# State times w_in as eight 64x32 tiles of the array, two banks at a time, in a fused attention and snake-MLP kernel

## The chip, the cores and the metric

The kernel runs on one core of a Trainium2 chip. The metric is the device time of one execution in microseconds (us); the median of three runs of the kernel before is 277.63 us.

## The reference

Eight batches (B), eight heads (H), 512 tokens (S), a state of 32 rows (Ns) per head, head width 64 (D). Each head's tokens attend over its state rows, and its state rows attend over its tokens; the two results are laid side by side to 8 x 544 = 4352 rows of 512 channels and go through an MLP of width 2048 whose activation is h + sin(alpha h)^2 / alpha.

```python
scores = scale * np.matmul(x, state.transpose(0, 1, 3, 2))
a = np.exp(scores - scores.max(-1, keepdims=True))
a /= a.sum(-1, keepdims=True) + 1e-09
xread = np.matmul(a, state)
...                                   # scores2, a2: state over x
sread = np.matmul(a2, x)
attn = np.concatenate([xread, sread], axis=2)   # then (B*S', H*D)
h = x @ w_in
s = np.sin(alpha * h)
g = h + s * s / (alpha + 1e-09)
return g @ w_out
```

Inputs and output are float32; the kernel works in bfloat16 with float32 sums.

## The kernel before

**Folding w_in into the state.** For the token rows, xread @ w_in is the softmax weights times (state @ w_in). So for each batch the kernel first makes M = state times w_in: 256 rows (8 heads of 32 state rows, in two groups g of four heads, 128 partitions each) by 2048 columns, in `m_step`. Then `mm1` makes a 128x512 piece of h for one of 16 slices f of the 2048 columns from M and the transposed softmax weights AT, as two matmuls (one per g) added in PSUM. The state rows (`xs_all`) are kept for a last stage, t = 8, where `mm1` uses w_in itself.

**m_step before.** The state is held transposed in `stT`: 128 partitions are two heads of 64 channels, and the 64 columns of a head pair are block-diagonal (head r's channels hold its 32 state rows in their own 32 columns, zeros in the other's). One `m_step` takes one group g and one quarter fs of the columns and issues two matmuls, h = 0 and 1, of 128 rows by 64 columns of the array and 512 moving columns each, into the lower and the upper 64 partitions of one PSUM bank; then it copies the bank to M on ScalarE or VectorE. Eight `m_step`s make a batch's M.

**The loop.** Stage t runs 16 rounds, f = 0 to 15. In each round TensorE gets `mm1` for slice f of batch t (two matmuls), then one of the pieces of the next batch's attention that the tables `pe` put at that round, then `mm2` of the batch before, four matmuls of g @ w_out (from t = 1). ScalarE takes the sine of h, GpSimd squares it (`s2`), VectorE forms g from h and the square two rounds later (`snake`), which also frees the h bank: there are four of them (psH), so `mm1` of round f needs the snake of round f - 4. Everything is issued in the order in which the Python code runs (a manual schedule), so on each engine the order of the code is the order of work.

**The next batch's attention**, by round: transposes T of x at 0 and 1, scores S at 3 and 4, exponentials X after 4 (with a table load before and after on ScalarE), row sums and reciprocals `Rs` after 7 and 8, normalizations `N` on GpSimd after 8 and 9, transposes of the weights `AT_` at 12, and the eight `m_step`s at rounds 2, 8, 9, 10, 11, 13, 14 and 15. Batch t's own column sums and state rows (`W`, `Cs`) sit at 6 and 7, with a reciprocal rC and two products on VectorE. At the end of round 15 VectorE packs the batch after the next (`xp`). M copies alternate between ScalarE and VectorE from stage 1 on; in stage 0 and ahead of the loop all are on ScalarE.

**PSUM.** psX has two banks, taken in turn by T, S, W, `AT_` and `m_step`; psO has two for the output.

**Ahead of the loop** batch 0's attention and its eight `m_step`s run once, as the quarters of w_in arrive. The last stages (t = 7 and 8) have no next batch and so no `m_step`.

## Time and profile before

| what | value |
|---|---|
| median of 3 runs | 277.63 us (277.3 to 278.13) |
| the profiled execution | 277.65 us |
| its span, first to last instruction | 275.9 us |
| granted TensorE clock, mean | 0.952 of full speed |
| TensorE busy | 246.4 us, 89% |
| GpSimd, VectorE, ScalarE busy | 171.5, 166.2, 160.5 us |
| matmuls of `m_step` | 128, 27.6 us busy |

How to read it: the busy share of TensorE counts overlapping matmuls once, and a matmul's end is modelled. A share over the whole span mixes the start (waiting for inputs), stage 0 (no `mm2` yet), the six full stages and the tail, so the full stages are read by their own stretch of time. A clock of 1.00 is 2.4 GHz, of 0.50 is 1.2 GHz.

### The profile page before, as it was taken

The page shows a single profiled execution, that of the slowest core. Times are in us where ns is not written, and L with a number is a line of the kernel's source. Part 1 is how long each engine was busy: PE and PEld are TensorE (multiplying, and loading weights), DVE is VectorE, ACT ScalarE, POOL GpSimd, SP SyncE. Part 2 cuts the span into 40 slices and gives each one's busy share as a digit, 9 for nine tenths or more (in the row PEclk, how much of TensorE's full clock was granted, in tenths as well). Part 3 has the DMA queues.
Part 4 walks back from the last instruction along what each step waited for, and adds up shares of the span by engine and source line. Part 5 has one row for each costly group of instructions (what it writes and reads, how often), then busy time and mean ns, then how long its engine had stood idle before and what let it go on. Part 6 is the DMA issues. An engine that isn't in the chain of part 4 may idle for free.

```text
span 275.9 us, 4169 instructions
## 1 busy us (share of the span) xinstructions
PE 246.4 (89%) x1504; PEld 112.7 (41%) x1532; DVE 166.2 (60%) x267; ACT 160.5 (58%) x254; POOL 171.5 (62%) x183
## 2 busy tenths in 40 slices
PE   7568565899989998999899989999999999999991
PEld 2424311443444443544354435433443444455640
DVE  3724578547766676668675866587749675544310
ACT  2563966077557854685559654955495556654420
POOL 8704499146956596559645965497449658764410
PEclk9955979599999999999999999999999999999998
DMA  7999660014511261117101700171111112112112
GB/s 85 203 203 207 105 76 1 4 39 63 91 38 38 48 106 38 39 37 116 40 2 49 112 36 36 40 114 38 40 39 38 40 38 76 40 38 76 42 55 60
DMA packets 19781, 17.85 MB, mean 65 GB/s; under 512 B 2992, under 2 KB 15280, under 8 KB 19760
## 3 DMA queue, kind: packets, MB, share of 16 engines
q0 software_dynamic: 12704, 8.65, 22.1%
q1 hardware_dynamic: 7056, 8.92, 9.8%
q8 instruction: 12, 0.20, 0.3%
q14 instruction: 9, 0.07, 0.1%
HBM read 17.31 MB, written 8.91 MB: 95 GB/s over the span
## 4 chain that ended last, share of the span: by engine, by line
PE 68%; DVE 17%; DMA 5%; POOL 4%; issue 3%; ACT 1%; ACTq 0%; POOLq 0%
PE o_ps L294 36%; PE h_ps L268 16%; DVE gT L285 6%; DMA xnat<-in_x_dram 5%; PE m_ps L250 5%; PE x_ps L170 3%; DVE rC L234 3%; DVE xp L158 3%; PE h_ps L274 3%; DVE M L260 2%; POOL s L281 2%; DVE xs_all L237 2%; PE w_ps L216 2%; DVE R L193 2%; PE s_ps L180 1%
## 5 line engine op out<-in xcount | busy, mean ns | idle before, releaser
L281 POOL TENSOR_TENSOR s<-s 128x512 bf16<-128x512 bf16 (+1 forms) x144 | 141.6, 992 | 89.3 <-ACT s L279 89.0
L279 ACT ACTIVATE s<-h_ps,alpha_sb 128x512 bf16<-128x512 f32 (+1 forms) x144 | 94.2, 665 | 85.4 <-PE h_ps L268 64.6
L294 PE MATMUL o_ps<-w_out_sb,gT 128*128 128x512 bf16 x522 | 136.5, 383 | 1.2 <-issue 0.7
L285 DVE SCALAR_TENSOR_TENSOR gT<-s,inva_sb,h_ps 128x512 bf16<-128x512 bf16 (+1 forms) x144 | 100.0, 710 | 38.9 <-POOL s L281 38.5
L268 PE MATMUL h_ps<-AT,M 128*128 128x512 bf16 x250 | 77.6, 392 | 5.8 <-DVE gT L285 4.3
L294 PEld LDWEIGHTS <-gT 128*128 128x128 bf16 x544 | 47.1, 98 | 51.3 <-issue 12.0
L268 PEld LDWEIGHTS <-M 128*128 128x128 bf16 x256 | 24.8, 100 | 36.4 <-issue 11.2
L250 PE MATMUL m_ps<-w_in_sb,stT 128*64 128x512 bf16 x128 | 27.6, 433 | 3.2 <-ACT M L258 1.6
L300 ACT COPY o_sb<-o_ps 128x512 f32<-128x512 f32 x34 | 20.0, 588 | 13.5 <-PE o_ps L294 12.5
L258 ACT CAST M<-m_ps 128x512 bf16<-128x512 f32 x40 | 22.8, 580 | 2.6 <-PE m_ps L250 2.6
L260 DVE CAST M<-m_ps 128x512 bf16<-128x512 f32 x24 | 16.2, 674 | 10.6 <-PE m_ps L250 10.6
L170 PE MATMUL x_ps<-ident,xp 128*128 128x128 bf16 x128 | 11.5, 243 | 9.6 <-DVE xp L158 9.6
L250 PEld LDWEIGHTS <-stT 128*64 128x64 bf16 x128 | 7.4, 109 | 29.3 <-issue 26.4
L234 DVE RECIPROCAL rC<-w_ps 128x128 f32<-128x128 f32 x8 | 7.7, 958 | 17.3 <-PE w_ps L227 17.3
L173 DVE COPY xT<-x_ps 128x1024 bf16<-128x1024 bf16 x16 | 11.0, 691 | 11.0 <-PE x_ps L170 11.0
L199 POOL TENSOR_TENSOR A<-E,rR 128x512 bf16<-128x512 bf16 x15 | 15.6, 1039 | 0.7 <-DVE rR L194 0.7
L170 PEld LDWEIGHTS <-xp 128*128 128x128 bf16 x128 | 9.2, 110 | 16.0 <-DVE xp L158 13.6
L210 DVE COPY AT<-a_ps 128x1024 bf16<-128x1024 bf16 (+1 forms) x9 | 5.7, 633 | 9.4 <-PE a_ps L207 9.3
L193 DVE TENSOR_REDUCE R<-E 128x16 f32<-128x512 bf16 x16 | 10.8, 676 | 0.5 <-ACT E L189 0.5
L158 DVE COPY xp<-xnat 128x2048 bf16<-128x2048 bf16 (+1 forms) x9 | 8.6, 959 | 4.3 <-DMA xnat<-in_x_dram 4.3
L189 ACT ACTIVATE E<-s_ps 128x512 bf16<-128x512 f32 x16 | 8.8, 595 | 1.7 <-PE s_ps L180 1.6
L274 PE MATMUL h_ps<-xs_all,w_in_sb 128*128 128x256 bf16 x64 | 9.6, 273 | 0.0
(40 smaller groups left out, 105.2 us busy)
## 6 DMA issues: line engine op xcount, KB each, us to landing
out_dram<-o_sb SPq DMA_DIRECT2D x32, 256.0 KB, 2.2
xnat<-in_x_dram POOLq DMA_DIRECT2D x7, 512.0 KB, 8.4
w_in_sb<-in_moe_w_in_dram POOLq DMA_DIRECT2D x4, 512.0 KB, 10.0
w_out_sb<-in_moe_w_out_dram POOLq DMA_DIRECT2D x4, 512.0 KB, 19.0
xnat<-in_x_dram POOLq DMA_DIRECT2D x2, 256.0 KB, 5.7
out_dram<-o_sb SPq DMA_DIRECT2D x8, 64.0 KB, 1.7
st_nat<-in_state_dram POOLq DMA_DIRECT2D x1, 256.0 KB, 4.6
alpha_sb<-in_moe_alpha_dram SPq DMA_DIRECT2D x1, 8.0 KB, 3.3
```

Of the source, the lines that this page charges most:

```text
L158: nc.vector.tensor_copy(a.xp[:, :, hs, :], xnat_l[a.b][:, hs, :].rearrange("p h (i d) -> p i h d", i=C),)
L170: nc.tensor.transpose(tp[:, k, i * P:(i + 1) * P], a.pair(i, 2 * g + k), ident[:])
L250: nc.tensor.matmul(mp[h * 2 * Ns:(h + 1) * 2 * Ns, :], stT[:, b * G + g, h * 2 * Ns:(h + 1) * 2 * Ns], w_in_sb[:, 2 * g + h, fs * FW:(fs + ...
L258: nc.scalar.copy(dst, mp[:])
L260: nc.vector.tensor_copy(dst, mp[:])
L268: nc.tensor.matmul(hp[:, :n], Ms[t][:, g, f * P:(f + 1) * P], atts[t].AT[:, g, :], start=(g == 0), stop=(g == G - 1),)
L274: nc.tensor.matmul(hp[:, :n], w_in_sb[:, q, f * P:(f + 1) * P], xs_all[:, q, :], start=(q == 0), stop=(q == Q - 1),)
L279: nc.scalar.activation(s[:, :n], hp[:, :n], ACT.Sin, scale=alpha_sb[:, f:f + 1])
L281: nc.gpsimd.tensor_tensor(s2[:, :n], s[:, :n], s[:, :n], ALU.mult)
L285: nc.vector.scalar_tensor_tensor(gT[t][:, f, :n], s2[:, :n], inva_sb[:, f:f + 1], hp[:, :n], ALU.mult, ALU.add)
L294: nc.tensor.matmul(op[:], gT[t][:, ft, st * P:(st + 1) * P], w_out_sb[:, ft, :], start=(ft == 0), stop=(ft == FT - 1),)
L300: nc.scalar.copy(o_sb[:], op[:])
```

## The change

One `m_step` now takes one quarter fs of the columns for both groups: eight matmuls of 64 rows by 32 columns of the array, each one head's state rows times that head's 64 rows of w_in, into two banks, one per group. In group 1 the two heads of a pair land in each other's 32 partitions, so that the two 64-row halves that write the same 32 partitions write different banks. The rows of M for group 1 are then in swapped order, and the normalization `N` writes the softmax weights of group 1 in the same swapped order (a reversed axis in the output), so that AT matches. The zeros of `stT` are no longer read by `m_step`. There are four `m_step`s a batch, at rounds 9, 11, 13 and 15, each with two copies: group 0 on ScalarE, group 1 on VectorE from stage 1 on. Ahead of the loop two stand before the transposes of A and two behind.

```diff
--- before.py
+++ after.py
@@ -195,10 +195,19 @@
 
         def N(a, g, eng):
             E8 = a.E[:, g].rearrange("p c (h j) -> p (c h) j", j=Ns)
-            A8 = a.A[:, g].rearrange("p c (h j) -> p (c h) j", j=Ns)
-            eng.tensor_tensor(
-                A8, E8, a.rR[:, g].unsqueeze(2).to_broadcast([P, C * HH, Ns]), ALU.mult
-            )
+            rb = a.rR[:, g].unsqueeze(2).to_broadcast([P, C * HH, Ns])
+            if g == 0:
+                A8 = a.A[:, g].rearrange("p c (h j) -> p (c h) j", j=Ns)
+                eng.tensor_tensor(A8, E8, rb, ALU.mult)
+            else:
+                A8 = a.A[:, g].rearrange("p c (e r j) -> p (c e) r j", r=2, j=Ns)
+                eng.tensor_tensor(
+                    A8[:, :, ::-1, :],
+                    a.E[:, g].rearrange("p c (e r j) -> p (c e) r j", r=2, j=Ns),
+                    a.rR[:, g].rearrange("p (e r) -> p e r", r=2).unsqueeze(3)
+                    .to_broadcast([P, C * HH // 2, 2, Ns]),
+                    ALU.mult,
+                )
 
         def AT_(a, gs):
             tp = psX.tile([P, len(gs), S], BF16, name="a_ps", tag="px")
@@ -241,23 +250,30 @@
                     ALU.mult,
                 )
 
-    def m_step(b, k, on_act):
-        fs, g = k // G, k % G
-        if k == 0:
+
+
+    def m_step(b, fs, on_act):
+        if fs == 0:
             Ms[b] = apool.tile([P, G, DFF], BF16, name="M")
-        mp = psX.tile([P, FW], FP32, name="m_ps", tag="px")
+        mp = [psX.tile([P, FW], FP32, name="m_ps", tag="px") for _ in range(G)]
         for h in range(2):
-            nc.tensor.matmul(
-                mp[h * 2 * Ns:(h + 1) * 2 * Ns, :],
-                stT[:, b * G + g, h * 2 * Ns:(h + 1) * 2 * Ns],
-                w_in_sb[:, 2 * g + h, fs * FW:(fs + 1) * FW],
-                start=True, stop=True,
-            )
-        dst = Ms[b][:, g, fs * FW:(fs + 1) * FW]
-        if on_act:
-            nc.scalar.copy(dst, mp[:])
-        else:
-            nc.vector.tensor_copy(dst, mp[:])
+            for g in range(G):
+                for r in range(2):
+                    rows = slice(r * D, (r + 1) * D)
+                    c0 = h * 2 * Ns + r * Ns
+                    o0 = h * 2 * Ns + (r ^ g) * Ns
+                    nc.tensor.matmul(
+                        mp[g][o0:o0 + Ns, :],
+                        stT[rows, b * G + g, c0:c0 + Ns],
+                        w_in_sb[rows, 2 * g + h, fs * FW:(fs + 1) * FW],
+                        start=True, stop=True,
+                    )
+        for g in range(G):
+            dst = Ms[b][:, g, fs * FW:(fs + 1) * FW]
+            if on_act[g]:
+                nc.scalar.copy(dst, mp[g][:])
+            else:
+                nc.vector.tensor_copy(dst, mp[g][:])
 
 
     def mm1(t, f):
@@ -326,12 +342,12 @@
     a.N(0, nc.gpsimd)
     a.Rs(1)
     a.N(1, nc.vector)
-    for k in range(4):
-        m_step(0, k, True)
+    for k in range(2):
+        m_step(0, k, (True, True))
     a.AT_([0])
     a.AT_([1])
-    for k in range(4, 8):
-        m_step(0, k, True)
+    for k in range(2, 4):
+        m_step(0, k, (True, True))
     atts[1] = Att(1)
     atts[1].pack(0, 1)
 
@@ -359,8 +375,8 @@
             add(post, 8, n.Rs, 1)
             add(post, 9, n.N, 1, nc.gpsimd)
             add(pe, 12, n.AT_, [0, 1])
-            for k, s in enumerate((2, 8, 9, 10, 11, 13, 14, 15)):
-                add(pe, s, m_step, t + 1, k, t == 0 or k % 2 == 0)
+            for k, s in enumerate((9, 11, 13, 15)):
+                add(pe, s, m_step, t + 1, k, (True, t == 0))
         if t < B:
             s = 6 if t + 1 < B else 0
             add(pe, s, atts[t].W)
```

On TensorE, round 9 of stage 2. `stT` is the state, `m_ps` the bank of M, `h_ps` that of `mm1`, `o_ps` that of `mm2`. Before:

```order
L268 MATMUL h_ps_1070<-AT_528,M_583 128x512
L250 LDWEIGHTS stT_123
L250 MATMUL m_ps_1077<-w_in_sb_105,stT_123 64x512
L250 LDWEIGHTS stT_123
L250 MATMUL m_ps_1077<-w_in_sb_105,stT_123 64x512
L294 LDWEIGHTS gT_524
```

The same place with the change:

```order
L284 MATMUL h_ps_1109<-AT_560,M_763 128x512
L265 LDWEIGHTS stT_123
L265 MATMUL m_ps_1117<-w_in_sb_105,stT_123 32x512
L265 LDWEIGHTS stT_123
L265 MATMUL m_ps_1117<-w_in_sb_105,stT_123 32x512
L265 LDWEIGHTS stT_123
L265 MATMUL m_ps_1118<-w_in_sb_105,stT_123 32x512
L265 LDWEIGHTS stT_123
L265 MATMUL m_ps_1118<-w_in_sb_105,stT_123 32x512
...
L310 LDWEIGHTS gT_556
```

The pair into one bank has become eight matmuls into two banks (the second four, left out, repeat these for the other two head pairs); rounds 2, 8, 10 and 14 have lost theirs.

On VectorE, from the row sums after round 7 to the snake of round 8 of stage 2. `R`, `rR` are row sums and their reciprocals, `gT` rows are snakes, `M<-m_ps` rows the copies of M. Before:

```order
L193 TENSOR_REDUCE R_866<-E_863 128x16
L194 RECIPROCAL rR_867<-R_866 128x16
L260 CAST M_920<-m_ps_1057 128x512
L285 SCALAR_TENSOR_TENSOR gT_861<-s2_997,inva_sb_125,h_ps_992 128x512
L193 TENSOR_REDUCE R_866<-E_863 128x16
L194 RECIPROCAL rR_867<-R_866 128x16
L285 SCALAR_TENSOR_TENSOR gT_861<-s2_1026,inva_sb_125,h_ps_1021 128x512
L260 CAST M_920<-m_ps_1094 128x512
L285 SCALAR_TENSOR_TENSOR gT_861<-s2_1055,inva_sb_125,h_ps_1050 128x512
```

With the change:

```order
L193 TENSOR_REDUCE R_914<-E_911 128x16
L194 RECIPROCAL rR_915<-R_914 128x16
L301 SCALAR_TENSOR_TENSOR gT_909<-s2_1040,inva_sb_125,h_ps_1035 128x512
L193 TENSOR_REDUCE R_914<-E_911 128x16
L194 RECIPROCAL rR_915<-R_914 128x16
L276 CAST M_1116<-m_ps_1118 128x512
L301 SCALAR_TENSOR_TENSOR gT_909<-s2_1069,inva_sb_125,h_ps_1064 128x512
L301 SCALAR_TENSOR_TENSOR gT_909<-s2_1098,inva_sb_125,h_ps_1093 128x512
```

The copy of M that stood ahead of the snake of round 6 stands ahead of the snake of round 7, and the one that stood behind that snake is gone to a later round.

## Rows read from the trace of the kernel before

**Rows 1.** The page, engines: busy us, share of the span, instructions.
```profile
PE 246.4 (89%) x1504; PEld 112.7 (41%) x1532; DVE 166.2 (60%) x267; ACT 160.5 (58%) x254; POOL 171.5 (62%) x183
```

**Rows 2.** Windows: stretch, length, busy us (instructions) per engine, clock, DMA, GB/s.
```profile
core 0: us, PE busy (x) PEld busy (x) DVE busy (x) ACT busy (x) POOL busy (x), PEclk, DMA share, GB/s
107.20:135.50 28.30, 27.11 (x173) 11.98 (x176) 19.44 (x32) 18.29 (x28) 19.27 (x20) 1.00 0.27 56
```

**Rows 3.** Timeline of VectorE, stage 3, rounds 7 to 9: start us, us, engine, line.
```profile
120.59 0.96 DVE L234 RECIPROCAL rC<-w_ps 128x128 f32<-128x128 f32 x1 [2.39 <-PE w_ps L227]
...
123.59 0.25 DVE L194 RECIPROCAL rR<-R 128x16 f32<-128x16 f32 x1
123.76 0.63 DVE L260 CAST M<-m_ps 128x512 bf16<-128x512 f32 x1
124.30 0.73 DVE L285 SCALAR_TENSOR_TENSOR gT<-s,inva_sb,h_ps 128x512 bf16<-128x512 bf16 x1
...
125.83 0.66 DVE L285 SCALAR_TENSOR_TENSOR gT<-s,inva_sb,h_ps 128x512 bf16<-128x512 bf16 x1
```

**Rows 4.** Chain of waits, end of stages 2 and 3: start us, us, what.
```profile
108.59 0.62 PE x_ps L170 x8
...
134.75 0.69 DVE M L260
...
136.09 0.73 DVE xp L158
136.88 0.62 PE x_ps L170 x8
```

**Rows 5.** Timeline of several engines in stage 0.
```profile
21.56 0.69 DVE L158 COPY xp<-xnat 128x2048 bf16<-128x2048 bf16 x1 [4.28 <-DMA xnat<-in_x_dram]
...
24.85 1.06 PE L268 MATMUL h_ps<-AT,M 128*128 128x512 bf16 x2
...
26.41 1.03 PE L268 MATMUL h_ps<-AT,M 128*128 128x512 bf16 x2
...
41.52 7.01 POOL L281 TENSOR_TENSOR s<-s 128x512 bf16<-128x512 bf16 x7
```

**Rows 6.** Chain of waits in stage 7, two rows of a pattern.
```profile
230.03 0.86 PE o_ps L294 x4
230.89 0.43 PE h_ps L268 x2
```

**Rows 7.** Timeline of TensorE, stage 3, rounds 9 to 12.
```profile
123.08 0.59 PE L268 MATMUL h_ps<-AT,M 128*128 128x512 bf16 x2
123.60 0.41 PE L250 MATMUL m_ps<-w_in_sb,stT 128*64 128x512 bf16 x2
123.94 1.04 PE L294 MATMUL o_ps<-w_out_sb,gT 128*128 128x512 bf16 x4
125.08 0.59 PE L268 MATMUL h_ps<-AT,M 128*128 128x512 bf16 x2
...
126.82 0.59 PE L268 MATMUL h_ps<-AT,M 128*128 128x512 bf16 x2
...
128.99 0.61 PE L207 MATMUL a_ps<-ident,A 128*128 128x128 bf16 x8
```

**Rows 8.** Groups by line and form: count | busy us, mean ns of one | idle before.
```profile
L281 POOL TENSOR_TENSOR s<-s 128x512 bf16<-128x512 bf16 x128 | 131.8, 1040 | 78.9 <-ACT s L279 78.7
L250 PE MATMUL m_ps<-w_in_sb,stT 128*64 128x512 bf16 x128 | 27.6, 433 | 3.2 <-ACT M L258 1.6 <-DMA w_in_sb<-in_moe_w_in_dram 1.0 <-ACT E L189 0.2
L199 POOL TENSOR_TENSOR A<-E,rR 128x512 bf16<-128x512 bf16 x15 | 15.6, 1039 | 0.7 <-DVE rR L194 0.7
L227 PEld LDWEIGHTS <-ones 128*64 128x64 bf16 x64 | 2.1, 109 | 3.4 <-issue 3.4
```

**Rows 9.** Timeline of TensorE's weight loads, column sums of stage 3.
```profile
120.11 0.26 PEld L227 LDWEIGHTS <-ones 128*64 128x64 bf16 x8 [0.42 <-issue]
```

**Rows 10.** Timeline of GpSimd: the second normalization of stage 3.
```profile
127.71 1.04 POOL L199 TENSOR_TENSOR A<-E,rR 128x512 bf16<-128x512 bf16 x1
```

## The prediction

> **What bounds the kernel now.** I read the page first: TensorE is busy 89% of the span, the next engine 62% [rows 1]. Then I read the stretches: in one warm batch (28.30 us) TensorE is busy 27.11 us at granted clock 1.00 (2.4 GHz), VectorE 19.44, GpSimd 19.27, ScalarE 18.29 [rows 2]. So a warm batch is a TensorE batch, and the chain of waits shows where it is not: each batch has two detours over VectorE. One runs from the reciprocal of the column sums (round 7) through snake steps, row sums and an M copy to the h matmul of round 10, which starts as soon as the snake of round 6 is through [rows 3, 7]. The other closes the batch: M copy, snake, pack of xp, and only then the transposes, from 134.75 to 136.88 us [rows 4]. Batch 0 is different: from 41.52 us on GpSimd runs seven squares without a gap, and VectorE and TensorE wait for it [rows 5]. So TensorE time removed in rounds 8 to 15 of batch 0 buys nothing.
>
> **What the change removes and adds on TensorE.** A matmul of 512 columns that follows another costs 0.216 us: four of mm2 take 0.86 us in batch 7, two of mm1 take 0.43 us [rows 6]. In round 9 of the warm batch, mm1 starts at 123.08 and mm2 at 123.94 us, 0.86 us apart [rows 7]. Two mm1 matmuls take 0.43 of it, so a w_in pair costs 0.43 us: one stream of 0.216, for its two halves run side by side (pairs start together, and the 128 of them keep TensorE busy 27.6 us where 128 times 433 ns would be 55 [rows 8]), and 0.21 us for changing the array's form there and back. A batch has eight pairs, 3.44 us. The new step does two pairs' work; if its eight tiles run side by side it pays one stream and one change of form, and a small delay for six more tiles.
>
> No row shows tiles of 64 rows, so that delay is bounded. From below: a pair keeps TensorE busy 0.41 us [rows 7] where one of its halves lasts 433 ns in the mean over warm and cold [rows 8], so the halves start almost together. From above: the eight small weight loads of the column sums take 0.26 us in all [rows 9] and 109 ns each [rows 8], so they start 0.02 us apart, and six more make 0.13 us. Further up: if the two row halves take turns, one more stream, 0.22 us. I take 0.03 us, nearest to the pair, because it is the same line in the same place. Call the delay d; a step costs 0.43 + d, four steps 1.72 + 4d, and the bare saving is 1.72 - 4d, or 1.60 us a batch.
>
> **What of it lies on the path.** I go through one warm batch (2.4 GHz), with the steps in their new rounds.
>
> Round 2: a pair is gone and nothing comes in its place. Everything after it up to round 7 (scores, exponentials, table loads, the squares that follow) hangs on TensorE's progress there, so all moves up by 0.43 us.
>
> Rounds 8 to 11: four pairs become two steps, so TensorE alone would gain 0.8 us. But VectorE's row of work between the reciprocal of round 7 and the snake of round 7 holds the same instructions as before: one M copy has moved from before the snake of round 6 to before the snake of round 7. So that snake starts where it did, at 125.83 us. The snake of round 6 started at 124.30 and its h matmul at 125.08, 0.78 us later [rows 3, 7]; so round 11's h matmul, which needs round 7's snake for its buffer, starts at 125.83 + 0.78 = 126.61 instead of 126.82. Gain 0.21 us, and not more. The step of round 9 is hidden here: TensorE has room until 126.6. Round 8's M copy gone from VectorE lets round 10 start earlier (0.54 us), and that is taken back in round 11.
>
> Rounds 11 to 12: the step of round 11 costs d more than the pair there did. Round 12's transposes of A then start about 0.18 us earlier than 128.99 [rows 7], 128.81 us. Their second half needs the last normalization on GpSimd, 127.71 + 1.04 = 128.75 us [rows 10]; GpSimd's chain starts from the scores, so it moves with round 2 and not with round 11. Room: some 0.06 us for the first transpose, and the four transposes of the first half before the others. No stall, but no room either.
>
> Rounds 13 to 15: step, nothing, step for three pairs. Round 13 loses d, round 14 gives 0.43 us, round 15 loses d, since the M copy, snake, pack and transposes hang on its end as they do now (2.13 us from M copy to transposes [rows 4]); that stall stays.
>
> Sum for a warm batch: 0.43 + 0.21 + 0.43 - 3d = 1.07 - 3d = 0.98 us with d = 0.03. Batches 1 to 6 have such steps (the transposes of successive batches are 28.29 us apart now [rows 4]; 27.3 expected): 5.9 us.
>
> Batch 0: the opening transposes wait for x, which lands so that the pack starts at 21.56 us [rows 5]; the four steps ahead of the loop, however fast, end before that. From there the pair of round 2 goes away at granted clock 0.50 (1.2 GHz): mm1 of round 2 starts at 24.85 and that of round 3 at 26.41 us, 1.56 apart [rows 5] where two streams of twice 0.216 are 0.86, so up to 0.70 us. Scores, table load and GpSimd's run follow. The clock rises in this stretch, and what moves ahead of the rise runs slow, so I take 0.5 us, with bounds 0 and 0.7. Batch 7 and the tail have no such step: nothing.
>
> **What moves but costs nothing.** M copies: eight a batch as before, four each on ScalarE and VectorE (two of 0.6 us run at once now). A step needs both psX buffers at once. In rounds 9 and 11 their last readers are done a round earlier. The tightest are round 12, whose buffer is freed by ScalarE's M copy of round 11, and round 13, whose second buffer is freed by the copy of AT: by my estimate from the same timeline a few tenths of a us ahead. If that cover went, TensorE would wait there for what is missing. The second half's normalization writes the pairs swapped: seven on GpSimd, one on VectorE ahead of the loop. GpSimd takes 1039 ns for the plain form, whose operand is broadcast, and 1040 for the plain square [rows 8], so I take 1.04 us; the bound above is twice that, the bound below a little gain that nothing could use.
>
> **Sum.** 5.9 + 0.5 = 6.4 us off the profiled execution's 277.65 us (span 275.9, and 1.75 around it; the median is 277.63, the same): **271.2 us**.
>
> **Rivals.** (A) The row halves do not share a bank. In the new step the upper and the lower 64 rows write different quadrants of the same two banks at once. If such writes take turns, the eight tiles in program order become five streams (first; second with third; fourth with fifth; sixth with seventh; last), d = 4 x 0.216 = 0.86. The step of round 9 stays nearly hidden (it would put round 11 at 126.55, against 126.61), the others do not: 1.07 - 3 x 0.86 = -1.51 us a batch, 9.1 us lost, less 0.5 in batch 0: 286.2 us. Slower from d = 0.36 us on. For it: no row here shows two row tiles. Against it: column halves share a bank now and run side by side [rows 7]. The Trainium skill, TensorEngine Tiling (Array Packing), Restrictions and Gotchas, says that different row tiles cannot access the same PSUM bank simultaneously, which speaks against this change as a whole; PSUM — Partial Sum Buffer, under bank collisions, narrows the fault it measured to one bank and one quadrant, and here no quadrant of a bank gets two row tiles. By the first page the time would be rival A's, by the second the forecast's; the trace cannot decide, and the change's pairing of heads keeps to the second.
>
> (B) The row halves take turns for another reason, d = 0.22: 0.41 us a batch, 2.5 us, with 0.5 of batch 0: 274.7 us. For it: such tiles are unseen here; against: column tiles start together.
>
> (C) GpSimd's swapped write takes twice the time. The second half of round 12's transposes then waits until 129.79, about 0.95 us, and the batch gains nothing: 277.1 us, no change. Against it: the two forms that GpSimd runs now cost the same.
>
> (D) VectorE's rounds 7 to 11 don't bind as tightly as I read: the bare 1.60 us a batch, 9.6 + 0.5 us: 267.5 us.
>
> **Chances.** Forecast 0.60; B 0.15; D 0.09; A 0.08; C 0.08. The range from 268.0 to 275.0 holds the forecast with both ends of d (0.13 gives 0.68 us a batch, 273.1), batch 0's bounds, B, and a little of D. It leaves out A, C and most of D. A measurement of this kernel can tell about 0.3% from no change (0.8 us). Faster: forecast, B and D less a small part that lands near zero, 0.82; same: 0.08; slower: 0.10.
>
> **What would show it.** Right: m_ps matmuls in groups of eight with starts within 0.1 us and about 0.86 us from mm1 to mm2 in rounds 9, 11, 13 and 15; transposes of successive batches 27.3 us apart; round 11's h matmul starting 0.8 us after VectorE's snake of round 7; the second normalization at 1.04 us. Wrong: mm1 to mm2 near 1.1 us in those rounds (B) or 1.7 us (A); the second normalization near 2 us and transposes of A waiting for it (C); a warm batch of 26.7 us (D); or TensorE waiting for M or AT copies ahead of a step.

## The result, and the profile after

The changed kernel takes **265.83 us** (median of 4 runs, 265.33 to 266.25) where the kernel before takes 277.86 (4 runs, 277.30 to 278.13): ratio 0.9569, 95% interval 0.9545 to 0.9592. That is 12.0 us less; the prediction said 6.4 less (271.2 us), and its range ended at 268.0. The sign was right, the size was not, and the time lies outside the range. The profiled execution of after took 265.33 us.

The page of after, with its span, the busy time of each engine (beside [rows 1]) and the granted clock in 40 slices:

```profile
span 263.5 us, 4423 instructions
PE 231.6 (88%) x1630; PEld 110.2 (42%) x1660; DVE 164.2 (62%) x267; ACT 160.0 (61%) x254; POOL 171.8 (65%) x183
PEclk9856968999999999999999999999999999999997
```

The clock row of the page of before, for comparison:

```profile
PEclk9955979599999999999999999999999999999998
```

In the eighth slice of before (48 to 55 us) stands a 5, half speed; in after there is none behind stage 0.

**Where the time went, stage by stage.** In the chain of waits each stage begins with the transposes of x. Those of after (start us, us, what), beside [rows 4, 5]:

```profile
22.35 1.03 PE x_ps L170 x8
...
45.97 0.62 PE x_ps L170 x8
...
73.23 0.62 PE x_ps L170 x8
...
100.50 0.62 PE x_ps L170 x8
...
127.76 0.62 PE x_ps L170 x8
```

And the first three of before, of which [rows 4] hold only the later ones:

```profile
22.31 1.03 PE x_ps L170 x8
...
49.14 1.03 PE x_ps L170 x8
...
80.30 0.62 PE x_ps L170 x8
```

| stage | before, us | after, us | gain | forecast |
|---|---|---|---|---|
| 0 | 26.83 | 23.62 | 3.21 | 0.5 |
| 1 | 31.16 | 27.26 | 3.90 | 0.98 |
| 2 and 3, each | 28.29 | 27.27 | 1.02 | 0.98 |

Stages 4 and 5 are like 2 and 3, and from stage 6's T to the end of the span after takes 1.16 us less. With stage 6 taken like the others the stages add up to 12.2 us. So the six warm terms came out as forecast (1.02 for 0.98), and the other 6.1 us, where 0.5 was forecast, came from two places that come once: stage 0 and the slow clock in stage 1.

**The warm batch.** TensorE in rounds 9 to 11 of stage 3 of after, the timeline (start us, us, engine, line), beside [rows 7]:

```profile
114.47 0.59 PE L284 MATMUL h_ps<-AT,M 128*128 128x512 bf16 x2 [0.21 <-DVE gT L301]
115.00 0.41 PE L265 MATMUL m_ps<-w_in_sb,stT 64*32 64x512 bf16 x8
115.34 1.04 PE L310 MATMUL o_ps<-w_out_sb,gT 128*128 128x512 bf16 x4
...
118.14 0.59 PE L284 MATMUL h_ps<-AT,M 128*128 128x512 bf16 x2 [0.47 <-DVE gT L301]
```

Eight tiles take 0.41 us, and `mm2` starts 0.34 us after the first of them and 0.87 us after `mm1`. A pair took 0.41, 0.34 and 0.86 [rows 7]. So the eight tiles cost what two did: d is 0.00 to within these rows' 0.01 us. By line, all of `m_step`'s matmuls (count, then busy us, mean ns of one, idle before), beside the second line of [rows 8]:

```profile
L265 PE MATMUL m_ps<-w_in_sb,stT 64*32 64x512 bf16 x256 | 16.3, 422 | 2.2 <-ACT M L274 2.0
```

27.6 us of TensorE's time became 16.3. VectorE in the same rounds, beside [rows 3], and the second normalization on GpSimd, beside [rows 10]:

```profile
115.27 0.75 DVE L301 SCALAR_TENSOR_TENSOR gT<-s,inva_sb,h_ps 128x512 bf16<-128x512 bf16 x1
...
116.81 0.63 DVE L276 CAST M<-m_ps 128x512 bf16<-128x512 f32 x1
117.36 1.39 DVE L301 SCALAR_TENSOR_TENSOR gT<-s,inva_sb,h_ps 128x512 bf16<-128x512 bf16 x2
```

```profile
119.18 1.04 POOL L204 TENSOR_TENSOR A<-E,rR 128x512 bf16<-128x512 bf16 x1
```

The snake of round 7 starts at 117.36 us and round 11's `mm1` at 118.14, 0.78 us later, the very step that the prediction used. The swapped write takes 1.04 us, as the plain one. What TensorE lost in waiting stands in the waits (us in total, times, longest), after and then before:

```profile
PE h_ps L284 <- DVE gT L301: 9.3, 20, 2.4
```

```profile
PE h_ps L268 <- DVE gT L285: 4.3, 5, 2.1
```

A warm batch now keeps TensorE busy for 25.50 of 27.27 us, before for 27.26 of 28.29 (windows from one T to the next; the other warm windows of before have down to 27.05): some 1.7 us of work went, and some 0.7 of it came back as waiting, mostly for VectorE's snakes by the rows above. Windows of before (stage 2) and of after (stage 3), in the columns of [rows 2]:

```profile
80.30:108.59 28.29, 27.26 (x174) 11.98 (x177) 19.42 (x31) 18.20 (x29) 19.26 (x19) 1.00 0.26 56
```

```profile
100.50:127.77 27.27, 25.50 (x189) 11.89 (x193) 19.50 (x31) 18.20 (x29) 19.23 (x19) 1.00 0.28 59
```

**Stage 0's end.** VectorE's pack of the next x, in before and in after:

```profile
46.24 2.85 DVE L158 COPY xp<-xnat 128x2048 bf16<-128x2048 bf16 x1
```

```profile
45.05 0.86 DVE L158 COPY xp<-xnat 128x2048 bf16<-128x2048 bf16 x1
```

The pack starts 1.23 us earlier, counted from each execution's own first T, and is 1.99 us shorter: 3.22 us, the whole gain of stage 0. The same copy takes 0.69 us at the start [rows 5]. In before it lasts while GpSimd's squares run on without a gap until 48.53 us [rows 5], and ends 0.56 us behind the last of them.

Most of the 1.23 us belongs to these two executions and not to the kernels. The granted clock rises from 0.50 to 1.00 early in stage 0, and other traces of the same code have the rise at another time. Three of the experiments below leave stage 0 of before as it is (5 and 9 stage 1 too), and two leave that of after:

| execution | clock rises, us behind T | pack starts, us behind T | pack, us | stage 0, us | stage 1, us |
|---|---|---|---|---|---|
| before | 5.4 | 23.93 | 2.85 | 26.83 | 31.16 |
| experiment 3, stage 0 as before | 4.1 | 23.31 | 2.85 | 26.21 | |
| experiment 5, both as before | 3.1 | 22.93 | 2.85 | 25.83 | 29.96 |
| experiment 9, both as before | 3.4 | 23.08 | 2.85 | 25.98 | 29.97 |
| after | 2.6 | 22.70 | 0.86 | 23.62 | 27.26 |
| experiment 10, stage 0 as after | 2.7 | 22.70 | 0.86 | 23.63 | |
| experiment 6, stage 0 as after | 5.1 | 23.41 | 0.90 | 24.37 | |

So the pack's two lengths go with the code, and up to 1.0 us of stage 0 and 1.2 of stage 1 go with the execution. The rows of experiment 5 behind its line of the table:

```profile
22.55 1.03 PE x_ps L170 x8
...
48.38 0.62 PE x_ps L170 x8
...
78.34 0.62 PE x_ps L170 x8
```

**The clock in stage 1.** Windows of before and of after (us, then PE, PEld, DVE, ACT, POOL busy, granted clock, DMA share, GB/s):

```profile
48.00:50.00 2.00, 0.86 (x9) 0.86 (x10) 1.08 (x1) 0.00 (x0) 0.53 (x1) 0.56 0.00 0
50.00:52.00 2.00, 1.78 (x6) 0.72 (x6) 1.35 (x2) 0.00 (x0) 0.00 (x0) 0.50 0.03 8
52.00:54.00 2.00, 2.00 (x12) 1.31 (x11) 0.37 (x1) 0.69 (x1) 0.40 (x1) 0.50 0.01 4
54.00:56.00 2.00, 2.00 (x9) 0.57 (x7) 2.00 (x4) 0.23 (x1) 0.64 (x1) 0.73 0.00 0
```

```profile
48.00:50.00 2.00, 2.00 (x15) 1.05 (x13) 1.63 (x3) 0.95 (x2) 1.04 (x1) 1.00 0.01 4
```

Ahead of this stand TensorE's waits for `xp` (us in total, times, longest), before and after:

```profile
PE x_ps L170 <- DVE xp L158: 9.6, 8, 3.2
```

```profile
PE x_ps L170 <- DVE xp L158: 7.5, 8, 1.3
```

Before, TensorE stood for 3.2 us ahead of this T, its longest wait of the kind, and then worked at 1.2 GHz until about 55 us. After, it stood for 1.2 us and went on at 2.4 GHz.

### The profile page after: what moved, and what is told of

The parts are those of the page before. It is cut to its first block, busy times and chain, and to the rows that moved or that the text cites. A ratio compares the mean times of both kernels' runs of the same rounds, so it can differ in the third digit from the quotient of the medians.

```text
span 263.5 us, 4423 instructions
## 1 busy us (share of the span) xinstructions
PE 231.6 (88%) x1630; PEld 110.2 (42%) x1660; DVE 164.2 (62%) x267; ACT 160.0 (61%) x254; POOL 171.8 (65%) x183
## 4 chain that ended last, share of the span: by engine, by line
PE 63%; DVE 21%; DMA 5%; POOL 4%; issue 3%; ACT 1%; ACTq 0%; POOLq 0%
PE o_ps L310 35%; PE h_ps L284 15%; DVE gT L301 8%; DMA xnat<-in_x_dram 5%; PE x_ps L170 3%; DVE R L193 3%; DVE rC L243 3%; PE h_ps L290 3%; DVE M L276 3%; PE m_ps L265 2%; POOL s L297 2%; DVE xp L158 2%; DVE xs_all L246 2%; PE w_ps L225 2%; DVE rR L194 1%
## 5 line engine op out<-in xcount | busy, mean ns | idle before, releaser
L284 PE MATMUL h_ps<-AT,M 128*128 128x512 bf16 x247 | 76.5, 390 | 9.7 <-DVE gT L301 9.3
L310 PEld LDWEIGHTS <-gT 128*128 128x128 bf16 x544 | 48.6, 98 | 50.9 <-issue 5.5
L265 PE MATMUL m_ps<-w_in_sb,stT 64*32 64x512 bf16 x256 | 16.3, 422 | 2.2 <-ACT M L274 2.0
L170 PE MATMUL x_ps<-ident,xp 128*128 128x128 bf16 x128 | 10.5, 231 | 7.5 <-DVE xp L158 7.5
L170 PEld LDWEIGHTS <-xp 128*128 128x128 bf16 x128 | 8.5, 104 | 13.5 <-DVE xp L158 11.5
L265 PEld LDWEIGHTS <-stT 64*32 64x32 bf16 x256 | 4.3, 90 | 17.6 <-issue 15.1
```

What stands on the lines that cost most here:

```text
L170: nc.tensor.transpose(tp[:, k, i * P:(i + 1) * P], a.pair(i, 2 * g + k), ident[:])
L265: nc.tensor.matmul(mp[g][o0:o0 + Ns, :], stT[rows, b * G + g, c0:c0 + Ns], w_in_sb[rows, 2 * g + h, fs * FW:(fs + 1) * FW], start=True, st ...
L284: nc.tensor.matmul(hp[:, :n], Ms[t][:, g, f * P:(f + 1) * P], atts[t].AT[:, g, :], start=(g == 0), stop=(g == G - 1),)
L310: nc.tensor.matmul(op[:], gT[t][:, ft, st * P:(st + 1) * P], w_out_sb[:, ft, :], start=(ft == 0), stop=(ft == FT - 1),)
```

## The experiments

The experiments ran on three chips, on which the kernel before took 272.98 to 278.46 us (45 runs, medians of 276.77, 277.17 and 277.21; 25 of the runs at 277 or above, like the profiled one, the others spread below). That is more scatter than the effects at stake in the smaller experiments, so these are read stage by stage, from one T to the next, in one profiled execution each; the medians stand beside. By their times alone, 8 and 10 are shown to be over 2% faster than the kernel before on their chip; 1, 4 and 12 are unclear by that measure, 2, 3, 7 and 11 the same, and 6 has no ratio. Stages 0 and 1 are compared with the first trace of before and with experiments 5 and 9, whose stages 0 and 1 are those of before.

**1. The old pairs in the new rounds.** Two pairs of the old form stand in each of the rounds of the new steps; nothing else of the change is in.

```diff
-            for k, s in enumerate((2, 8, 9, 10, 11, 13, 14, 15)):
+            for k, s in enumerate((9, 9, 11, 11, 13, 13, 15, 15)):
```

> The kernel before with its pairs of 128x64 tiles, but two pairs each in rounds 9, 11, 13 and 15 instead of one in eight rounds. It separates the new rounds from the new tiles. Theory (the forecast's formula holds in warm batches, 1.07 - 3d, and two pairs in a row mean d = 0.43 us): a warm batch takes 28.5 us, 0.2 more than before; stage 0 gains about 1.2 us from the empty round 2, as in the changed kernel. Time 277.8 us if stage 0's pack of xp still takes 2.85 us, about 273 if it takes 0.8 as in the changed kernel. Rival (the rounds do the work, not the tiles): a warm batch of 27.3 to 27.6 us and a time of 266 to 268.

Measured: 270.06 us (269.24 to 272.72). Stages 23.98, 27.79 and then 27.78 us; the pack 1.21 us, no drop of the clock in stage 1. TensorE's timeline around one double step:

```profile
116.20 0.59 PE L268 MATMUL h_ps<-AT,M 128*128 128x512 bf16 x2 [0.21 <-DVE gT L285]
116.72 0.62 PE L250 MATMUL m_ps<-w_in_sb,stT 128*64 128x512 bf16 x4
117.28 1.04 PE L294 MATMUL o_ps<-w_out_sb,gT 128*128 128x512 bf16 x4
```

So neither expectation for the warm batch was right. From `mm1` to `mm2` it is 1.08 us with two pairs and 0.86 with one: the second pair costs its stream, 0.22 us, and not a second change of the array's form. With 0.22 in the place of d the prediction's formula gives 28.29 - (1.07 - 3 x 0.22) = 27.88 us, against 27.79. Of the 1.02 us that a warm batch gains, the rounds alone bring 0.50, the eight tiles 0.52. And the rounds alone bring most of both one-off gains: 2.85 us in stage 0 and 3.37 in stage 1 against the first trace of before, 1.85 and 2.17 against experiment 5.

**2. The kernel before, its pack in stage 0 by another operation.** A maximum of x with itself, in two halves, in the place of the copy.

```diff
+        def pack_tt(a, g):
+            hs = slice(g * H // 2, (g + 1) * H // 2)
+            src = xnat_l[a.b][:, hs, :].rearrange("p h (i d) -> p i h d", i=C)
+            nc.vector.tensor_tensor(a.xp[:, :, hs, :], src, src, ALU.max)
...
-                atts[b].pack(0, 1)
+                if b == 2:
+                    atts[b].pack_tt(0)
+                    atts[b].pack_tt(1)
+                else:
+                    atts[b].pack(0, 1)
```

> The kernel before, its stage 0 pack of xp done as two halves by VectorE with a maximum of x and x instead of a copy; all else as before. Theory (the 2.85 us of that one copy came from GpSimd's run of squares next to it, and the low clock at the start of stage 1 from the wait that followed): each half takes 1.1 to 1.2 us whatever GpSimd does, the transposes of stage 1 start near 47.4 instead of 49.1 us, the clock stays at 1.00 through stage 1, and the time falls by 1.7 + 2.9 us to about 273.2. Rival 1 (the copy is slow for another reason, such as late data): the halves are late too, no change, 277.9. Rival 2 (the clock would have fallen anyway): only 1.7 us less, 276.2.

Measured: 275.63 us (273.96 to 278.11). The two halves as one row:

```profile
45.44 3.45 DVE L166 TENSOR_TENSOR xp<-xnat 128x1024 bf16<-128x1024 bf16 x2
```

The first half took 2.84 us of it and the second 0.68 (they overlap a little), so the maximum waits just as the copy does; the theory that it would not is refuted. Stage 0 takes 25.88 and stage 1 29.96 us, with the clock at 0.50 from 50 to 52 us. That is less than in the first trace of before, but experiments 5 and 9 have the same lengths with the plain copy, so no gain of this edit is shown.

**3. The kernel before, TensorE kept busy in the gap.** Thirteen matmuls on zeros, into two psX banks that nothing else uses then, during the wait for stage 1's first T. The pack is as it was.

```diff
+            if t == 1:
+                def keep_busy():
+                    fp = psX.tile([P, FW], FP32, name="f_ps", tag="px")
+                    for _ in range(12):
+                        nc.tensor.matmul(fp[:], warm[:, 0:P], warm[:], start=True, stop=True)
...
+                add(pe, 0, keep_busy)
             add(pe, 0, n.T, 0)
```

> The kernel before, with 13 matmuls of zeros by zeros on TensorE (into spare PSUM banks, nothing reads them) while it waits for the pack ahead of stage 1; the wait itself stays. Theory (the fall of the clock after that wait costs about 2.9 us in stage 1): the clock stays at 1.00 in stage 1, its transposes start at 49.1 to 49.3 us as before, stage 1 takes 28.3 instead of 31.2 us, time about 275.0. Rival (stage 1 is long for other reasons than the clock): stage 1 near 31 us, time 277.9 or a little more.

Measured: 274.66 us (273.77 to 275.29), in the profiled execution 274.33. Pack 2.85 us as before, and stage 1 takes 28.29 us in the place of 31.16, which is the length of a warm batch:

```profile
48.73 0.62 PE x_ps L170 x8
...
77.02 0.62 PE x_ps L170 x8
```

The windows of this run show the clock at 1.00 from 48 us on:

```profile
48.00:50.00 2.00, 1.63 (x14) 0.86 (x13) 1.28 (x2) 0.00 (x0) 0.12 (x1) 1.00 0.03 8
```

So the low clock behind the wait costs 2.9 us against the first trace of before, where stage 1 ran some 6 us at it, and 1.7 against experiments 5 and 9, where it ran some 3.5 us at it. The wait itself comes on top, and stage 1 holds nothing else that a warm batch does not.

**4. The kernel after, its pack in stage 0 held back** until GpSimd has squared the first slice of stage 1.

```diff
...
+        if t == 1:
+            atts[2] = Att(2)
+
+            def late():
+                nc.vector.tensor_copy(tiny2[:], last_s2[0][:, 0:1])
+                atts[2].pack(0, 1)
+            add(pe, 0, late)
...
-            add(post, 15, nxt)
+            if t != 0:
+                add(post, 15, nxt)
...
```

> The changed kernel, with stage 0's pack of xp held back until GpSimd has finished the first square of stage 1, so that the copy runs after GpSimd's run and TensorE waits some 2.4 us more. Theory: the copy takes 0.8 us or a little more, the transposes of stage 1 start near 48.4 instead of 46.0 us, the clock falls to 0.50 in stage 1 and stage 1 takes about 30 us: 265.8 + 2.4 + 2.9 = 271.1 us, which is what was forecast for the change. Rival 1 (the wait costs but not the clock): 268.2. Rival 2 (stages 0 and 1 gained from the new tiles themselves): 266 to 267.

Measured: 271.73 us (270.02 to 272.61). Stages 26.58, 29.93, and then 27.27 us: 2.96 and 2.67 us given back by the first two, nothing by the warm ones. Window of this run:

```profile
52.00:54.00 2.00, 2.00 (x7) 0.63 (x6) 1.02 (x2) 0.00 (x0) 0.00 (x0) 0.50 0.00 0
```

A late pack alone brings back the clock's hole and puts the change at about the time that I had forecast. (In this trace the clock rose 4.7 us behind T, and by the table above a rise that late is up to 0.75 of the 2.96 us.) So experiments 3 and 4 show where the missed gain lay: in the pack and in the clock behind it.

**5. The copy against GpSimd, by itself.** Behind the end of the kernel before stand eight blocks of six GpSimd products of 128x512, each with a copy of the pack's size on VectorE, released by the first product and set back by none, one or two row sums (0.68 us each); in some blocks ScalarE feeds the products.

```diff
...
+        for i in range(6):
+            src = warm[:]
+            if chained:
+                nc.scalar.copy(pa[:, i, :], last[:, i % 4, :])
+                src = pa[:, i, :]
+            nc.gpsimd.tensor_tensor(pq[:, i, :], src, src, ALU.mult)
+            if i == 0:
...
+                nc.vector.tensor_copy(now, w_out_sb[:, 0:4, :])
...
```

> The kernel before with eight probes behind its last stage; the output is untouched. In each probe GpSimd runs six 128x512 products in a row (about 1.0 us each; in four of the probes each waits for a ScalarE copy that runs ahead of it), and VectorE, once the first is through, does nothing, one or two row sums of 0.68 us, and then a 128x2048 copy within SBUF like the pack of xp. Theory 1 (GpSimd keeps the way to SBUF as long as its next instruction is ready): every copy ends only after the sixth product, 2.5 to 5 us long, and shorter the later it starts; with the ScalarE waits it gets in earlier where a product is not ready in time. Theory 2 (the copy waits for the product that runs and is then let in, and stage 0's long copy has another cause): every copy takes 0.8 to 1.6 us and one product is stretched by some 0.5 us, as in the changed kernel.

Measured (320.17 us with the added blocks): two of the copies, and the products beside the first of them.

```profile
283.28 1.44 DVE L411 COPY pd<-w_out_sb 128x2048 bf16<-128x2048 bf16 x1
...
290.67 0.85 DVE L411 COPY pd<-w_out_sb 128x2048 bf16<-128x2048 bf16 x1
```

```profile
282.14 6.47 POOL L404 TENSOR_TENSOR pq<-pa 128x512 bf16<-128x512 bf16 x6
```

The copy waits for the product under way and then gets in: 1.44 us where it is asked for 0.15 us into a product, 0.85 where 0.73 us into one, never 2.85. (The pack of before is asked for 0.73 us into a square.) Six products take 6.47 us where six of the seven squares of [rows 5] take 6.0, so one product in turn waits some 0.45 us for the copy. The Trainium skill, SBUF — State Buffer, Who interferes with whom, says that a VectorE copy in a two-port mode and a GpSimd instruction exclude each other for a whole instruction, whichever starts first, and that a tensor_tensor with both inputs in SBUF contends too. The probe's 0.85 to 1.44 us agree, and so does experiment 2's 2.84 us in kind; that one copy stood behind the square under way and two more is not told by that rule.

**6. The kernel after with its pack a round earlier** in the warm stages.

```diff
-            add(post, 15, nxt)
+            add(post, 15 if t == 0 else 14, nxt)
```

> The changed kernel with the pack of xp one round earlier (14 instead of 15) in all stages but stage 0, which leaves its copy ahead of the M copy that waits for the last step. Theory (the 0.77 us that the transposes of each warm batch wait comes from M copy, snake and pack in a row): the wait goes, a warm batch takes 26.5 instead of 27.27 us, time 265.8 - 6 x 0.77 = 261.2 us. Rival (the copy then meets GpSimd's run of squares and waits as in stage 0 of the kernel before): copies of 1.5 to 3 us, a warm batch of 27.3 us or more, 266 to 270.

Measured: two runs at 261.3 and 261.5 us, two at 265.3 and 266.4; the profiled one is 261.5, and what the longer two lost is not shown. Its stages: 24.37, then 26.34 and 26.33 us. The wait ahead of T, which the prediction said would stay and which did stay, is worth 0.94 us a batch, once the pack no longer stands behind round 15.

**7. The kernel before with only round 2 emptied.**

```diff
-            for k, s in enumerate((2, 8, 9, 10, 11, 13, 14, 15)):
+            for k, s in enumerate((8, 8, 9, 10, 11, 13, 14, 15)):
```

> The kernel before, pairs as they are, with the pair of round 2 alone moved to round 8 (two pairs there). Theory: stage 0 comes 1.2 us earlier to its pack of xp, as in the changed kernel, and a warm batch gains 0.43 us in round 2 and gives 0.2 back in round 8, 28.1 us: about 275 us if the pack still takes 2.85 us, about 270 if it takes 0.8 to 1.2 us and the clock stays up. Rival (stage 0's gain came from the new steps of rounds 9 to 15): stage 0 as before, 26.8 us from its first transposes to those of stage 1, 277.

Measured: 274.20 us (271.74 to 275.10). Stage 0 takes 25.63 us; the pack still takes its long time:

```profile
45.15 2.85 DVE L158 COPY xp<-xnat 128x2048 bf16<-128x2048 bf16 x1
```

Stage 1 takes 30.5 us at a low clock, a warm batch 27.94. So an empty round 2 does not let the pack in. Its worth is not 1.20 us, the difference from the first trace of before: experiments 5 and 9, with a rise of the clock nearer to this one's (3.6 us behind T), are only 0.20 and 0.35 us longer. The plainest pair are experiments 6 and 8, alike up to round 2 and with the rise at 5.1 and 5.3 us: stage 0 takes 24.37 us with that round empty and 24.81 with a step in it, so 0.44 us.

**8. The kernel after with its steps in rounds 2, 9, 11 and 13,** so that no M copy stands ahead of the last snake.

```diff
-            for k, s in enumerate((9, 11, 13, 15)):
+            for k, s in enumerate((2, 9, 11, 13)):
```

> The changed kernel with its eight-tile steps in rounds 2, 9, 11 and 13 instead of 9, 11, 13 and 15. Theory (the sum of the forecast with d = 0): in a warm batch round 2 gains nothing, rounds 8 to 11 give 0.2, rounds 13 to 15 give 0.86 us, and with no M copy in round 15 the wait of the next transposes (0.77 us) goes: 26.5 us a batch. Stage 0 loses the 1.2 us of its empty round 2. About 262 us if stage 0's pack gets through in 0.8 to 1.2 us, 267 if it takes 2.85 us and the clock falls. Rival (only the number of steps matters, not the rounds): a warm batch of 27.3 us and 266 us.

Measured: 263.55 us (262.45 to 264.02), stage 0 24.81 us with a pack of 0.90, warm batch 26.42 us. It is as good as experiment 6: the end of the batch is a chain of M copy, snake and pack, and either of the two moved out of it gives some 0.9 us.

**9. The probe with longer runs:** four blocks of fourteen products in a row, with the copy released by the tenth. The edit, against experiment 5's block:

```diff
-        for i in range(6):
+        for i in range(14):
...
-            if i == 0:
+            if i == 9:
```

> The kernel before with four probes behind its last stage, as in the probe run ahead of this, but with fourteen GpSimd products in a row and VectorE's copy asked for after the tenth (at once, or after one row sum), twice with products that nothing holds up and twice with products that follow ScalarE copies running ahead. Theory A (after a long run without a gap GpSimd keeps the way until the run ends): the copy lasts 3 to 4.5 us. Theory B (a copy waits for the product under way alone, long run or short): 0.8 to 1.5 us, and what held the copy of stage 0 is something that the probes lack.

Measured: copies of 1.44, 0.85, 1.44 and 0.85 us. A long run of GpSimd without a gap does not by itself hold the copy back for more than one product.

**10. All of it together:** the pack at round 14, the steps in rounds 2, 9, 11 and 14, the weights' transposes at 13, both M copies of round 9 on ScalarE; stage 0 stays as in after.

```diff
-            add(pe, 12, n.AT_, [0, 1])
-            for k, s in enumerate((9, 11, 13, 15)):
-                add(pe, s, m_step, t + 1, k, (True, t == 0))
+            add(pe, 12 if t == 0 else 13, n.AT_, [0, 1])
+            for k, s in enumerate((9, 11, 13, 15) if t == 0 else (2, 9, 11, 14)):
+                add(pe, s, m_step, t + 1, k, (True, t == 0 or s == 9))
...
-            add(post, 15, nxt)
+            add(post, 15 if t == 0 else 14, nxt)
```

> The changed kernel with stage 0 as it is, and in stages 1 to 6 steps in rounds 2, 9, 11 and 14, both M copies of round 9 on ScalarE, the transposes of A in round 13 and the pack of xp after round 14. Theory (the two detours over VectorE are what keeps a warm batch from TensorE's own time): the snake of round 7 starts 0.55 us earlier, the wait of the transposes of x is gone, a warm batch takes about 26.0 us, time 265.8 - 6 x 1.25 = 258.3 us. Rival (GpSimd's normalization or ScalarE's copies take their place): 26.4 us or more a batch, 261 or more.

Measured: **258.10 us** (257.34 to 258.40), ratio to the kernel before on the same chip 0.9345, interval 0.928 to 0.941. It beats both kernels, though after (265.83) was not run beside it. The window of one of its batches:

```profile
72.90:98.67 25.77, 25.56 (x195) 11.86 (x194) 19.30 (x31) 18.69 (x30) 19.31 (x20) 1.00 0.29 62
```

TensorE is busy for 25.56 of 25.77 us. Against before (27.26 of 28.29) that is some 1.7 us of work and some 0.8 of the 1.0 us of waiting less, all of it time.

**11. The kernel before with ScalarE held up in stage 0:** three more copies of M by ScalarE in round 13, so that GpSimd's squares get a gap near the pack.

```diff
             nc.scalar.copy(dst, mp[:])
+            if b == 1 and k == 5:
+                for _ in range(3):
+                    nc.scalar.copy(dst, mp[:])
```

> The kernel before, with ScalarE made to copy one M piece of stage 0, round 13, three times more, so that the sine of round 14 comes about 1.1 us later and GpSimd's square of that round has to wait for it. Theory (the pack gets in only where GpSimd's run has just been interrupted by a wait for ScalarE): the copy takes 0.8 to 1.3 us instead of 2.85, the clock stays up, and although ScalarE has more to do the time falls to 272.5 to 273.5 us. Rival (the interruption has nothing to do with it): copy 2.85 us, 277 to 278.5 us.

Measured: 274.76 us (272.23 to 276.00), in the profiled execution 272.47, so the median is above what I expected and the traced run is not. By the times the kernel is the same as before on that chip (ratio 0.9948, interval 0.9894 to 1.0003), and what the longer runs lost is not shown. The traced run's pack:

```profile
45.40 0.69 DVE L158 COPY xp<-xnat 128x2048 bf16<-128x2048 bf16 x1
```

Stages 24.12, 28.27 and 28.29 us: with a gap on GpSimd the pack takes 0.69 us and the clock stays up. Against experiments 5 and 9 that is 1.7 to 1.9 us of stage 0 and 1.7 of stage 1 (2.7 and 2.9 against the first trace of before), with more work done and with the old tiles in the old rounds.

**12. The kernel after with half of stage 0's M copies on VectorE,** so that ScalarE's sines run ahead as in before.

```diff
-                add(pe, s, m_step, t + 1, k, (True, t == 0))
+                add(pe, s, m_step, t + 1, k, (True, False))
```

> The changed kernel, with half of stage 0's M copies on VectorE as in the later stages instead of all on ScalarE, so that ScalarE's sines of rounds 14 and 15 run ahead of GpSimd. Theory (as for the kernel before with the late sine): GpSimd runs without a gap into the pack, the copy takes 2 to 2.9 us, the clock falls in stage 1, 269 to 271 us. Rival: copy below 1.3 us, 265 to 266.5 us.

Measured: 268.91 us (267.32 to 269.81), but not in the expected way. The pack takes 0.75 us and starts at 47.61 us, 2.6 later than in after, behind VectorE's own copies; stage 0 takes 26.20 and stage 1 28.76 us, with the clock at 0.53 from 48 to 50 us though TensorE's wait ahead of it was 1.6 us. What I meant to test, whether sines ahead of GpSimd keep the pack out, was not tested by this.

## Why the prediction was wrong, point by point

**Right: the cost of the step.** The 0.43 + d with d near that of a pair: d is 0.00, for the 0.03 taken. Experiment 1 confirms the split into 0.22 for the stream and 0.21 for the change of form from the other side: a second pair behind the first costs only the 0.22. Rival A (row halves take turns on a bank, d = 0.86) and rival B (d = 0.22) are out by the same rows. The Trainium skill, TensorEngine Tiling (Array Packing), Restrictions and Gotchas, has row tiles unable to access one bank at once; eight tiles that write two banks from both row halves in the time of a pair contradict that as long as each 32-partition quadrant of a bank has one writer.

**Right: what of it lies on the path in a warm batch.** 0.43 + 0.21 + 0.43 - 3d is 1.07 with the measured d, 1.02 was measured. The steps hold one by one: round 11 starts 0.78 us behind the snake of round 7, the wait ahead of T is 0.77 us in both traces, GpSimd's swapped write is 1.04 us. Rival C needed twice that. Rival D (VectorE does not bind, 1.60 us a batch) is out: TensorE's waits for snakes rose from 4.3 to 9.3 us. Experiments 6, 8 and 10 show that it was right for its reason: take M copy or pack out of that chain and the batch loses another 0.9 us, take out all and it loses 1.5.

**Wrong: "Batch 0 ... I take 0.5 us, with bounds 0 and 0.7".** Measured 3.21 between the two traces. The term itself, the empty round 2, was sized well: 0.44 us (experiments 6 and 8). What failed is that it stood alone, on the sentence "TensorE time removed in rounds 8 to 15 of batch 0 buys nothing". It buys the pack. With the pairs of rounds 9 to 15 where they were, and round 2 empty, the pack takes 2.85 us (experiment 7); with them in rounds 9, 11, 13 and 15 it takes 1.21 (experiment 1), with the new steps there 0.86. The prediction has no term for it, though the copy's row of 2.85 us at the end of stage 0, where a warm batch has 0.73 [rows 4], was there to be seen; 2.0 us of it went away. The rest of the 3.21, some 0.8 us, is luck, of the execution and not of the kernel: the clock rose 2.8 us earlier behind T in the trace of after. Windows of before and of after, then of experiment 5 (stage 0 as before) and experiment 6 (stage 0 as after):

```profile
24.00:27.00 3.00, 3.00 (x15) 1.41 (x14) 1.99 (x4) 1.74 (x3) 1.33 (x2) 0.50 1.24 209
```

```profile
24.00:27.00 3.00, 2.67 (x25) 1.83 (x24) 1.99 (x4) 1.96 (x3) 1.70 (x2) 0.84 1.24 207
```

```profile
24.00:27.00 3.00, 3.00 (x25) 1.65 (x23) 1.99 (x4) 1.69 (x3) 1.27 (x2) 0.72 1.24 209
```

```profile
24.00:27.00 3.00, 3.00 (x19) 1.75 (x18) 1.98 (x4) 1.42 (x3) 1.18 (x2) 0.50 1.24 207
```

The code of before gets 0.50 or 0.72 there, that of after 0.84 or 0.50, so no trace shows the early rise to be the change's doing; with the late one stage 0 of after takes 0.75 us more (24.37, experiment 6).

**Wrong: "Batches 1 to 6 have such steps ... 5.9 us".** Stage 1 was counted as a warm batch. It took 31.16 us and a warm one 28.29 before; the 2.9 us of difference are the low clock behind the long wait (experiment 3; 1.7 us in experiments 5 and 9), and they went with the wait. So the sum was 5.9 + 0.5 = 6.4, and measured were 6 x 1.02 = 6.1, 3.2 and 2.9: 12.2. With stage 0 and stage 1 of before as in experiment 5 and stage 0 of after as in experiment 6 it would be 5 x 1.02, 25.83 - 24.37 = 1.46 and 29.96 - 27.26 = 2.70: 9.3 us, an estimate. So that the two terms are missing is a fault of the prediction, and some 3 us of their size hang on when the clock happened to change.

**What stays open** is why the pack waits for the square under way and two more in before and in experiments 2, 3, 5, 7 and 9, and for one at most in after and in experiments 1, 6, 8 and 10. One thing separates these two groups without exception. In the first, the square of round 14, which is under way when the pack is asked for, started 0.36 to 0.70 us after its sine was done; in the second it had just waited for its sine and started 0.08 us after it. Sine and square, in before and in after:

```profile
44.13 0.69 ACT L279 ACTIVATE s<-h_ps,alpha_sb 128x512 bf16<-128x512 f32 x1 [0.43 <-PE h_ps L268]
...
45.51 1.03 POOL L281 TENSOR_TENSOR s<-s 128x512 bf16<-128x512 bf16 x1
```

```profile
43.54 0.71 ACT L295 ACTIVATE s<-h_ps,alpha_sb 128x512 bf16<-128x512 f32 x1
...
44.33 1.04 POOL L297 TENSOR_TENSOR s<-s 128x512 bf16<-128x512 bf16 x1
```

In that second group ScalarE has two M copies of round 13 ahead of that sine, in before one. Experiment 11, with three more copies there, got the pack in too, but by leaving GpSimd idle when the pack came, as did experiment 4 (0.68 us). So that the change lets the pack in is shown, and that the steps' new rounds do it, not the empty round 2 and not the tiles (experiments 1 and 7). That ScalarE's two copies are the reason fits every trace of stage 0 but is not shown: the probes' products let the copy in without such a wait (experiments 5 and 9), and experiment 12 missed its aim.

## What to carry to other kernels

Price the first stages apart from the warm ones: compare the length of each stage in the chain with the steady one, and ask of every surplus (here 2.9 us in stage 1 and a copy of 2.85 us where its like take 0.7 to 0.8) what keeps it there and whether the change touches that. Before calling a difference in such a stage the change's, look at a second trace of the same code: here the clock's rise alone moved stage 0 by up to 1.0 us. A wait that is long enough to lower the clock costs twice, and a small shift that shortens it can give back more than the work that the change removes. And when a change frees the busiest engine, look at once for the chain that ends next: moving the pack and M copies out of it and spacing the steps anew was worth more here (1.5 us a batch) than the warm term of the change itself (1.02).

## What the runs showed of the hardware

- Eight tiles of 64 rows by 32 columns, into two banks, take the time of two tiles of 128 by 64 into one: 0.41 us, and 0.34 from the start of the first to the next matmul.
- Going to another tile form and back costs 0.21 us once, by the difference of these rows, however many matmuls of that form stand together (0.86 us from `mm1` to `mm2` with one pair, 1.08 with two).
- A TensorE wait of 3.2 us was followed by some 6 us at 1.2 GHz, which cost 2.9 us, waits of 3.0 us by some 3.5 us at it, which cost 1.7 (experiments 5 and 9). After waits of 1.0 to 1.2 us the clock stayed at 2.4 GHz (after, experiments 1, 6, 8 and 10), with one of 1.6 us it fell (experiment 12).
- The rise of the granted clock from 0.50 to 1.00 (1.2 to 2.4 GHz) in stage 0 came 3.1 to 5.4 us behind T in four traces of the same code (before, experiments 3, 5 and 9), 2.6 to 5.1 us in three of the other (after, experiments 6 and 10).
- A VectorE copy of 128x2048 that takes 0.69 us alone takes 0.85 to 1.44 beside running GpSimd products, one of which loses 0.45 us, and in some programs 2.85; a maximum of two SBUF operands waits likewise (2.84 us for half the size).
- A write with a reversed axis costs GpSimd nothing: 1039 ns for both forms.
